# Delta-rule attention step: the result as two quarter-array products summed in PSUM, and every burst on two lanes of quarters

## The chip, the cores and the metric

The kernel runs on one core of a Trainium2 chip. The metric is device time in microseconds (us) of one execution, lower is better. TensorE (PE in the views) multiplies; VectorE (DVE), ScalarE (ACT) and GpSimd (POOL) do the elementwise work; SyncE (SP) starts most of the transfers. The 128x128 array of TensorE can be used as a whole or as four quarters of 64x64, each of which takes its own small product.

## The reference

Three stages in a row, all in fp32. Cut to what is computed:

```python
def _attn_ref(q, k, v, beta):            # (4 batches, 8 heads, 768 steps, 48)
    k_n = k / (norm(k) + 1e-06)
    state = zeros((B, H, D, D))
    for t in range(S):
        y[:, :, t] = einsum('bhd,bhde->bhe', q[:, :, t], state)
        v_old = einsum('bhde,bhd->bhe', state, kt)
        state = state + bt * einsum('bhd,bhe->bhde', kt, vt - v_old)

x = y.transpose(0, 2, 1, 3).reshape(3072, 384)

h = x @ w_in                              # MoE1: 384 -> 2048 -> 384
P = a[0] + a[1]*h + a[2]*h*h + a[3]*h*h*h
Q = 1.0 + abs(b[0])*abs(h) + abs(b[1])*h*h
x = (P / (Q + 1e-06)) @ w_out

h = x @ w_in                              # MoE2, own weights
r = maximum(h, 0.0)
return (r * r) @ w_out
```

## The kernel before, in words

**Attention.** The 768 steps of each batch are cut into 12 chunks of 64. A chunk of one batch is a "step" n = 4c + b (c the chunk, b the batch), 48 in all; eight steps form a group g = 0 to 5. The eight heads stand as four pairs p; the two heads j of a pair lie on rows 0 to 63 and 64 to 127 of a tile. Inside a chunk the recurrence is a triangular solve: a Gram matrix of the keys (`gram`), its inverse by 32x32 blocks (the loop of 31 steps, L497 and L501, on DVE for group 0 and on POOL for the others), and then for each step these products per pair and head:

- `kv`: keys times [queries | state], 64x112, into a PSUM tile H. Its left part is the scores, which are masked to a triangle; its right part is subtracted from the values (`cr`, L711).
- `tv`: inverse times the corrected values, 64x48, into U, which is copied out as the new values.
- the result Y: masked scores times new values, plus queries times state. Before, both lie below one another in a tile X, so that one product over 112 or 128 rows (`c3`, L727 for the one head, L728 for the other) forms the sum. X has two slots per batch, one per head, and zeros between the used rows.
- `ku`: keys times new values, 48x48, added to the state by DVE (`so`, L745).

`products` (L662) issues the quarter products of a burst two by two in turn from each kind. The scores are copied from PSUM head by head (`either`, which is ACT at L348 or DVE at L352, as the planner likes) and masked by POOL (L700); for chunk 1 alone DVE does copy and mask in one (L704).

**MoE1 and MoE2.** Six blocks i of 512 tokens by 16 tiles j of 128 hidden columns make 96 "units" in each. A unit of MoE1 is mm1 (L910, on split operands xh and xl), a rational function in 11 operations over ACT, DVE and POOL (L927 to L937, in this order of need: Abs, L928, L930 on POOL, L933, L934, L935, L936, L937; the cubic by `either` at L348 or L353, L931, L932, L935), and mm2 into three accumulators, either in fp32 (L958) or on split operands (L961, after L941 and L942). MoE2 has relu squared (L975 to L979) and L988 to L990.

**The order.** Nothing is scheduled by a compiler. A planner in the file (class `Plan`) takes every operation with an estimated duration, a due time (`tm(u)` = T0 + U1 u for unit u), reads, writes and a PSUM bank from a pool, runs a list schedule and issues every engine's instructions in the order found. Group 0 of the attention runs before MoE1; groups 1 to 5 run inside it, each as ten "bursts" t = 0 to 9, in which PE does `kv` of step t, `tv` of step t-1, the result and `ku` of step t-2 and, for the groups 1 to 3, one `gram` of a later group. Weights of MoE2 are prepared on DVE (L853, L861) and ACT in MoE1's last part. In idle stretches ahead of MoE1 the planner adds dummy products of `ones` (L303).

Of the kernel before, what the change touches and what calls it, by code (L numbers as in the profile page):

```python
# [19 lines left out]
C = 64  # L20
# [11 lines left out]
T0, U1, U2 = 88.0, 5.9, 4.15  # L32
# [213 lines left out]
def kernel(ctx, tc, kT, kS, qT, kn, vn, beta, par_in, w1, w2, outT):  # L246
# [13 lines left out]
    acc = banks[0:3]  # L260
    PL.pool("h", banks[3:6])
# [107 lines left out]
    for b in range(B):  # L369
        def xz(b=b):  # L370
            x = X[b]
            P_.memset(x[32:64, 1, :, 0:64], 0.0)
            P_.memset(x[64:128, 0, :, 64:112], 0.0)
            P_.memset(x[0:64, 1, :, 64:112], 0.0)
        add("POOL", 0.9, xz, w=[("q", b), ("q1", b), ("S", b)], due=10 + b, lock=1)

# [30 lines left out]
    for n in range(8):  # L407
# [42 lines left out]
    def attention(g):  # L450
# [36 lines left out]
        add("DVE", 2.2, r1, r=GB + ["nby", "be"], w=["nbr", "nrm"], due=d0, lock=1, after=turned if g == 1 else [])  # L487
        add("DVE", 0.2, lambda: V.transpose(nT[g % 2], nrm), r=["nrm"], w=[("nT", g % 2)], due=d0 + 2, lock=1)
        add("DVE", 1.3, lambda: V.tensor_tensor(Gb, Gb, _mid(nbr, [128, 32, 32]), op=ALU.mult), r=["nbr"], w=GB, due=d0, lock=1)
        add("DVE", 0.25, lambda: V.tensor_copy(Tt.rearrange("p a b -> p (a b)")[:, 0:1024:33], nbr), r=["nbr"], w=[tt], due=d0, lock=1)  # L490
        for s in range(31):
# [33 lines left out]
        if g < 2:  # L525
# [3 lines left out]
            add("POOL", 2.0, tz, w=[("TT", g)] + [("Dg", n) for n in range(8)] if g == 0 else [("kt0", q) for q in range(4)] + [("TT", 1)],  # L529
                due=d1 - 2, lock=1)  # L530
# [74 lines left out]
        def head(k):  # L605
# [20 lines left out]
        def kv(k):  # L626
# [17 lines left out]
        def ku(k):  # L644
# [480 lines left out]
```

## Time and profile before

| what | before |
|---|---|
| median of 3 runs | 1069.54 us (1068.82 to 1070.16) |
| profiled execution | 1065.81 us, its span 1064.1 us |
| mean granted clock of TensorE | 0.974 |
| PE busy | 1009.4 us of the span (95%) |
| DVE busy | 711.3 us (67%) |
| ACT busy | 625.6 us (59%) |
| POOL busy | 470.6 us (44%) |

The time of an execution is its span and what lies around it. Up to about 90 us PE does group 0 of the attention; MoE1 then runs to about 664 us and MoE2 to the end. Busy time of PE includes stretches at the lower of its two clocks: `PEclk` 1.00 is 2.4 GHz, 0.50 is 1.2 GHz, and a mean between them says which share of the stretch ran at either.

### The profile page before, as it was taken

Reading aid. Unit: us, or ns where it says so; the run is one execution under the profiler, and the core shown is the slowest. Engines: PE = TensorE matmul, PEld = TensorE weight load, DVE = VectorE, ACT = ScalarE, POOL = GpSimd, SP = SyncE. Lnnn points to the kernel's source line nnn. Section 1 sums busy time; section 2 is a strip of 40 time slices with the busy share of each in tenths; the row PEclk is TensorE's granted clock in tenths of the full one; section 3 lists DMA queues with packets and bytes.
Section 4 is the critical chain, followed back from the end, with each engine's and each line's share of the span. In section 5 each row is a group of like instructions: output and inputs, shape, how many; then the busy total and the mean of one; then the engine's idle time right before and its main releaser. Section 6 shows DMA issues by size and latency. Waiting matters only on the chain.

```text
span 1064.1 us, 22303 instructions
## 1 busy us (share of the span) xinstructions
PE 1009.4 (95%) x8932; PEld 755.7 (71%) x8932; DVE 711.3 (67%) x1154; ACT 625.6 (59%) x1126; POOL 470.6 (44%) x629
## 2 busy tenths in 40 slices
PE   5687998999999989999999898999999999999998
PEld 5575665567777766776766565888888888888886
DVE  4986888987898778778887998864343343433432
ACT  5364777777787877678776686753233242333322
POOL 3389999589868838873443453740000000000000
PEclk7978999999999999999999998999999999999999
DMA  7784367513731560251103113701010010000000
GB/s 245 185 214 104 86 185 228 88 36 104 169 72 38 148 104 34 67 127 37 28 9 123 59 60 127 259 1 59 1 30 30 1 60 1 1 30 1 30 0 30
DMA packets 126024, 85.44 MB, mean 80 GB/s; under 512 B 93344, under 2 KB 110880, under 8 KB 125920
## 3 DMA queue, kind: packets, MB, share of 16 engines
q1 hardware_dynamic: 125920, 84.02, 29.0%
q8 instruction: 70, 1.15, 0.4%
q14 instruction: 34, 0.28, 0.1%
HBM read 64.20 MB, written 18.61 MB: 78 GB/s over the span
## 4 chain that ended last, share of the span: by engine, by line
PE 72%; DVE 13%; POOL 7%; ACT 3%; issue 2%; DMA 2%; SPq 1%; POOLq 0%; DVEq 0%; ACTq 0%
PE bank L910 32%; PE bank L958 10%; PE bank L990 6%; PE bank L988 6%; PE bank L989 6%; PE bank L961 6%; PE bank L662 4%; POOL tmp L497 2%; POOL Tt L501 2%; PE bank L727 1%; DVE mem L937 1%; DVE mem L931 1%; DVE mem L932 1%; DVE mem L935 1%; DVE mem L353 1%
## 5 line engine op out<-in xcount | busy, mean ns | idle before, releaser
L910 PE MATMUL bank<-xh,A 128*128 128x512 f32 x1152 | 359.6, 393 | 1.0 <-POOL A L867 1.0
L910 PEld LDWEIGHTS bank<-xh,A 128*128 128x128 f32 x1152 | 218.2, 190 | 59.3 <-issue 11.3
L910 PE MATMUL bank<-xl,A 128*128 128x512 f32 x576 | 250.2, 434 | 6.6 <-DVE xl L894 3.4
L958 PE MATMUL bank<-mem,B 128*128 128x512 f32 x366 | 183.0, 621 | 17.4 <-DVE mem L937 17.4
L930 POOL TENSOR_TENSOR mem<-mem 128x512 f32<-128x512 f32 x96 | 125.4, 1306 | 110.9 <-ACT mem L928 108.9
L976 DVE SCALAR_TENSOR_TENSOR mem<-bank,mem 128x512 f32<-128x512 f32 x96 | 66.2, 690 | 147.4 <-ACT mem L975 147.3
L975 ACT ACTIVATE mem<-bank 128x512 f32<-128x512 f32 x96 | 57.4, 598 | 150.7 <-PE bank L910 150.7
L910 PEld LDWEIGHTS bank<-xl,A 128*128 128x128 f32 x576 | 109.3, 190 | 48.3 <-issue 10.4
L958 PEld LDWEIGHTS bank<-mem,B 128*128 128x128 f32 x366 | 68.2, 194 | 70.2 <-issue 41.8
L979 DVE TENSOR_TENSOR gl<-mem,gh 128x512 fp32r<-128x512 f32 x96 | 71.9, 749 | 65.4 <-ACT gh L978 65.3
L990 PE MATMUL bank<-gh,C 128*128 128x512 f32 x288 | 113.8, 395 | 0.0
L988 PE MATMUL bank<-gl,C 128*128 128x512 f32 x288 | 113.5, 394 | 0.0
L989 PE MATMUL bank<-gh,C 128*128 128x512 f32 x288 | 111.9, 389 | 0.0
L978 ACT CAST gh<-mem 128x512 fp32r<-128x512 f32 x96 | 59.6, 621 | 78.0 <-DVE mem L976 66.4
L501 POOL TENSOR_TENSOR Tt<-Tt,tmp 128x31 f32<-128x31 f32 (+15 forms) x155 | 88.0, 568 | 10.6
L497 POOL TENSOR_TENSOR tmp<-Gb,Tt 128x31 f32<-128x31 f32 (+15 forms) x155 | 84.6, 546 | 14.2 <-DVE Tt L490 4.6
L927 ACT ACTIVATE mem<-bank 128x512 f32<-128x512 f32 x96 | 57.1, 595 | 46.3 <-PE bank L910 24.2
L935 DVE SCALAR_TENSOR_TENSOR mem<-mem,par,bank 128x512 f32<-128x512 f32 x96 | 71.2, 742 | 17.5 <-ACT bank L934 16.5
L933 ACT ACTIVATE mem<-mem,par 128x512 f32<-128x512 f32 x96 | 69.2, 722 | 22.0 <-POOL mem L930 20.7
L928 ACT ACTIVATE mem<-mem,par 128x512 f32<-128x512 f32 x96 | 78.1, 814 | 2.7
L348 ACT COPY X<-bank 64x192 f32<-64x192 f32 (+1 forms) x176 | 59.3, 337 | 27.0 <-PE bank L662 12.4
L932 DVE SCALAR_TENSOR_TENSOR mem<-mem,par,bank 128x512 f32<-128x512 f32 x96 | 71.3, 744 | 4.3 <-ACT mem L927 1.9
(128 smaller groups left out, 1798.8 us busy)
## 6 DMA issues: line engine op xcount, KB each, us to landing
raw<-in_w_dram SPq DMA_DIRECT2D x18, 768.0 KB, 5.3
B<-in_w_dram SPq DMA_DIRECT2D x10, 768.0 KB, 5.7
kTg<-in_kS_dram SPq DMA_DIRECT2D x40, 128.0 KB, 2.6
gs<-Gs SPq DMA_DIRECT2D x40, 128.0 KB, 2.6
kTc<-in_kT_dram SPq DMA_DIRECT2D x40, 128.0 KB, 2.7
kn<-in_kn_dram SPq DMA_DIRECT2D x12, 384.0 KB, 3.9
X<-in_qT_dram SPq DMA_DIRECT2D x96, 48.0 KB, 2.8
vn<-in_vn_dram SPq DMA_DIRECT2D x12, 384.0 KB, 4.8
```

Source lines behind the costliest of these rows:

```text
L497: E_.tensor_tensor(tv, _mid(Gb[:, s, s + 1:32], [128, a, b]), Tt[:, 0:a, s:s + 1].to_broadcast([128, a, b]), op=ALU.mult)
L501: E_.tensor_tensor(Tt[:, 0:a, s + 1:32], Tt[:, 0:a, s + 1:32], tv, op=ALU.subtract)
L910: M.matmul(h, a, b, start=(k == 0 and m == 0), stop=(k == NK - 1 and m == 2))
L928: add("ACT", 0.83, lambda: A_.activation(b(), a(), AF.Identity, bias=s(4), scale=s(5)), r=[ak, "par"], w=[bk], due=due + 3.3, alloc=(("b", ...
L930: add("POOL", 1.32, lambda: P_.tensor_tensor(b(), b(), a(), op=ALU.mult), r=[ak], w=[bk], due=due + 4.2, lock=1)
L932: add("DVE", 0.75, lambda: V.scalar_tensor_tensor(c(), c(), s(1), h(), op0=ALU.add, op1=ALU.mult), r=[hk, "par"], w=[ck], due=due + 6.3)
L935: add("DVE", 0.75, lambda: V.scalar_tensor_tensor(c(), c(), s(0), h(), op0=ALU.add, op1=ALU.mult), r=[hk, "par"], w=[ck], due=due + 8)
L958: M.matmul(acc[d], Bw[j][:, e], slot[gk], start=(j == 0), stop=(j == NJ - 1))
L979: add("DVE", 0.72, lambda: V.tensor_tensor(gl(), b(), gh(), op=ALU.subtract), r=[bk, gk, "late"], w=[lk], due=due + 5, lock=1, alloc=(("gl ...
L988: M.matmul(acc[d], wh, gl, start=(j == 0), stop=False)
L989: M.matmul(acc[d], wl, gh, start=False, stop=False)
L990: M.matmul(acc[d], wh, gh, start=False, stop=(j == NJ - 1))
```

## The change

- **The result.** `c3` goes. In its place stand `mu` (new values times masked scores, 64 rows) and `qs` (state times queries, 48 rows), both quarter products, that add up in the same PSUM bank; only the first of a bank clears it.
- **X.** Slot 0 holds scores and new values of both heads, slot 1 queries and state. The zeros between go (12 memsets on POOL), the two query loads of a step become one of 112 KB, the two copies of U become one, the two additions to the state one.
- **The mask.** One DVE operation of 128x4x64 per step copies and masks the scores of both heads; the 88 maskings on POOL go.
- **The lanes.** `products` takes two lanes. `kv`, `tv` and `ku` use the quarters on the diagonal, `gram`, `mu` and `qs` the two others (the heads swap sides for that; the rows of w1 are permuted on the host). All products of a burst are issued in the order of their lane's columns so far. `gram` goes to the bank of Y, the state's product to that of U.
- **Planner.** U1 5.9 to 5.7, IV1 25 to 30, a factor SLOW 1.25 on the POOL inversion of group 1, SA 60 to 40 (the weights of MoE2 are prepared later), several durations; the last block's mm1 may also use the attention's banks, and its cubic always goes to ACT. The zeros of the second TT tile are copied by ACT from the first in place of two memsets.

```diff
-T0, U1, U2 = 88.0, 5.9, 4.15
+T0, U1, U2 = 88.0, 5.7, 4.15
+SLOW = 1.25
-IV1, WB, WS = 25, 44, 4.5
-SA, SB = 60, 4
+IV1, WB, WS = 30, 44, 4.5
+SA, SB = 40, 4
...
-                yield t[64:128, p, 0:w], kt[0:48, p], x[0:48, 1, p, 0:w]
-                yield t[0:64, p, 0:w], kt[64:112, p], x[64:112, 0, p, 0:w]
+                for o in (0, 64):
+                    yield t[o:o + 64, p, 0:w], kt[o:o + 48, p], x[o:o + 48, 1, p, 0:w]
...
-        def products(*gens):
-
-            gens = list(gens)
-            while gens:
-                for q in list(gens):
-                    for _ in range(2):
-                        y = next(q, None)
-                        if y is None:
-                            gens.remove(q)
-                            break
-                        M.matmul(*y, start=True, stop=True)
+        def products(*lanes):
+
+            seq = []
+            for q, lane in enumerate(lanes):
+                z = 0.0
+                for y in lane:
+                    z += y[0].free_size() if hasattr(y[0], "free_size") else y[0].shape[-1]
+                    seq.append((z, q, len(seq), y))
+            for *_, y in sorted(seq, key=lambda v: v[:3]):
+                a, z = y[3:] or (True, True)
+                M.matmul(*y[:3], start=a, stop=z)
...
-                add("POOL", 0.47, cm, r=["mark"] if c == 0 else [], w=[("M", b, j)], due=due + 0.5, lock=1)
+
+            def cp():
+                V.tensor_tensor(x[:, 0, :, 0:64], ps(hk, [128, NP, 112])[:, :, 0:64], _mid(tri, [128, NP, C]), op=ALU.mult)
+            add("DVE", 0.38, cp, r=[hk, "tri"], w=[("M", b)], due=due, free=[hk])
...
-        def c3(n):
+        def mu(k):
+            n = 8 * g + k
             t, x = yv(n), X[n % B]
             for p in range(NP):
-                M.matmul(t[0:48, p], x[0:112, 0, p, 64:112], x[0:112, 0, p, 0:64], start=True, stop=True)
-                M.matmul(t[64:112, p], x[:, 1, p, 64:112], x[:, 1, p, 0:64], start=True, stop=True)
+                for o in (0, 64):
+                    yield t[64 - o:112 - o, p], x[o:o + 64, 0, p, 64:112], x[o:o + 64, 0, p, 0:64], p == 0, n < B and p == NP - 1
+
+        def qs(k):
+            n = 8 * g + k
+            t, x = yv(n), X[n % B]
+            for p in range(NP if n >= B else 0):
+                for o in (0, 64):
+                    yield t[64 - o:112 - o, p], x[o:o + 48, 1, p, 64:112], x[o:o + 48, 1, p, 0:64], False, p == NP - 1
...
             def go():
-                if k2 is not None:
-                    c3(8 * g + k2)
-                products(*([kv(k0)] if k0 is not None else []), *([tv(k1)] if k1 is not None else []),
-                         *([ku(k2)] if k2 is not None else []), *([gram(m, slot["U", m - 16][:, NP * D:NP * (D + C)].rearrange("r (p c) -> r p c", p=NP))] if m else []))
+                products(chain(*([] if k0 is None else [kv(k0)]), *([] if k1 is None else [tv(k1)]), *([] if k2 is None else [ku(k2)])),
+                         chain(*([gram(m, slot["Y", g, t][:, NP * C:2 * NP * C].rearrange("r (p c) -> r p c", p=NP))] if m else []),
+                               *([] if k2 is None else [mu(k2), qs(k2)])))
...
-        either(0.78, 0.7, lambda: (c(), h()), s(2), s(3), r=[hk, "par"], w=[ck], due=due + 4.5, alloc=(("c",), ck))
+        if i == NT - 1:
+            add("ACT", 0.78, lambda: A_.activation(c(), h(), AF.Identity, bias=s(2), scale=s(3)), r=[hk, "par"], w=[ck], due=due + 4.5, alloc=(("c",), ck))
+        else:
+            either(0.78, 0.7, lambda: (c(), h()), s(2), s(3), r=[hk, "par"], w=[ck], due=due + 4.5, alloc=(("c",), ck))
```

What the new order looks like at three places (the names are those of the two programs; a tile's number only tells tiles apart).

POOL at the start of MoE1, before: the last steps of the inversion of group 1 (L497, L501), a weight (L867), the two memsets of TT (L528), and only then the first unit's product (L930).

```order
96 L497 TENSOR_TENSOR tmp_122<-Gb_118,Tt_120 128x60
97 L501 TENSOR_TENSOR Tt_120<-Tt_120,tmp_122 128x30x2
98 L497 TENSOR_TENSOR tmp_122<-Gb_118,Tt_120 128x31
99 L501 TENSOR_TENSOR Tt_120<-Tt_120,tmp_122 128x31
100 L867 TENSOR_TENSOR A_82<-mem,A_82 128x384
101 L528 MEMSET TT_115 32x32x32 x2
102 L930 TENSOR_TENSOR mem<-mem 128x512
```

POOL at the same place now (the inversion is L493 and L497, the unit's product L937):

```order
72 L493 TENSOR_TENSOR tmp_127<-Gb_123,Tt_125 128x156
73 L497 TENSOR_TENSOR Tt_125<-Tt_125,tmp_127 128x26x6
74 L937 TENSOR_TENSOR mem<-mem 128x512
75 L493 TENSOR_TENSOR tmp_127<-Gb_123,Tt_125 128x135
76 L497 TENSOR_TENSOR Tt_125<-Tt_125,tmp_127 128x27x5
77 L493 TENSOR_TENSOR tmp_127<-Gb_123,Tt_125 128x112
78 L937 TENSOR_TENSOR mem<-mem 128x512
```

The first two units' products have moved ahead of the last five steps of the inversion, and the memsets have left POOL there.

PE in a full burst of the groups 1 to 3, before: eight products of the result, then the quarters two by two.

```order
722 L727 MATMUL bank_73<-X_111 48x64
723 L728 MATMUL bank_73<-X_111 48x64
724 L727 MATMUL bank_73<-X_111 48x64
725 L728 MATMUL bank_73<-X_111 48x64
726 L662 MATMUL bank_76<-X_113,kTc_140 64x112 x2
727 L662 MATMUL bank_75<-vn_136,TT_115 64x48 x2
728 L662 MATMUL bank_73<-X_111,kn_134 48x48 x2
729 L662 MATMUL bank_75<-kTg_141 64x64 x2
```

PE in the same kind of burst now (all of it is L663):

```order
769 L663 MATMUL bank_74<-kTg_147 64x64 x2
770 L663 MATMUL bank_73<-X_115,kTc_142 64x112
771 L663 MATMUL bank_74<-kTg_147 64x64 x2
772 L663 MATMUL bank_73<-X_115,kTc_142 64x112
773 L663 MATMUL bank_74<-kTg_147 64x64
774 L663 MATMUL bank_73<-X_115,kTc_142 64x112
775 L663 MATMUL bank_74<-kTg_147 64x64 x2
776 L663 MATMUL bank_73<-X_115,kTc_142 64x112
777 L663 MATMUL bank_74<-X_117 48x64 x2
```

The products on whole rows are gone, and the two lanes alternate from the burst's first product on.

PE at the end of MoE1, before: the last units' mm2 (L961 on split operands, L958 in fp32), and behind all of them the first mm1 of MoE2 (L910 of A_79).

```order
2428 L961 MATMUL bank_71<-ph,F_2554 128x512
2429 L961 MATMUL bank_71<-ph,E_2547 128x512
2430 L958 MATMUL bank_69<-mem,B 128x512
2431 L958 MATMUL bank_70<-mem,B 128x512
2432 L958 MATMUL bank_71<-mem,B 128x512
2433 L910 MATMUL bank_76<-xl_99,A_79 128x512
2434 L910 MATMUL bank_76<-xh_96,A_79 128x512 x2
```

PE at the end of MoE1 now (mm1 is L914, mm2 L965 and L968):

```order
2854 L965 MATMUL bank_69<-mem,B 128x512
2855 L965 MATMUL bank_70<-mem,B 128x512
2856 L965 MATMUL bank_71<-mem,B 128x512
2857 L914 MATMUL bank_76<-xl_104,A_84 128x512
2858 L914 MATMUL bank_76<-xh_101,A_84 128x512 x2
2859 L914 MATMUL bank_76<-xl_105,A_84 128x512
2860 L914 MATMUL bank_76<-xh_102,A_84 128x512 x2
2861 L914 MATMUL bank_76<-xl_106,A_84 128x512
2862 L914 MATMUL bank_76<-xh_103,A_84 128x512 x2
2863 L968 MATMUL bank_69<-pl,E_2579 128x512
```

MoE2's first mm1 (A_84) now stands ahead of the last two units' mm2 of MoE1, and its second ahead of the last one's.

## Rows read from the trace of the kernel before

**Rows 1.** The page: span, and busy time of each engine.

```profile
span 1064.1 us, 22303 instructions
PE 1009.4 (95%) x8932; PEld 755.7 (71%) x8932; DVE 711.3 (67%) x1154; ACT 625.6 (59%) x1126; POOL 470.6 (44%) x629
```

**Rows 2.** Busy time of each engine by stretches; the first column is the stretch.

```profile
core 0: us, PE busy (x) PEld busy (x) DVE busy (x) ACT busy (x) POOL busy (x), PEclk, DMA share, GB/s
...
150.00:200.00 50.00, 45.42 (x585) 28.31 (x584) 45.17 (x73) 37.95 (x72) 38.86 (x53) 1.00 0.80 210
200.00:220.00 20.00, 17.96 (x179) 11.13 (x178) 19.03 (x32) 15.52 (x28) 15.19 (x22) 0.91 0.18 52
...
565.00:600.00 35.00, 31.01 (x106) 20.07 (x104) 26.53 (x40) 20.89 (x33) 10.29 (x8) 0.95 0.27 93
600.00:640.00 40.00, 38.88 (x143) 26.27 (x142) 39.17 (x56) 32.43 (x52) 21.77 (x18) 1.00 0.24 79
640.00:664.00 24.00, 19.79 (x59) 11.45 (x58) 21.06 (x30) 14.03 (x25) 8.72 (x8) 0.86 0.38 125
664.00:1064.00 400.00, 396.42 (x1728) 324.01 (x1726) 164.77 (x229) 151.49 (x255) 32.62 (x26) 1.00 0.11 36
```

**Rows 3.** Waits of PE from 88 to 660 us: total, times, longest.

```profile
PE bank L958 <- DVE mem L937: 17.4, 7, 4.6
```

**Rows 4.** Timeline of PE at MoE1's start: start, length, what, wait before.

```profile
90.00 0.79 PE L910 MATMUL bank<-xl,A 128*128 128x512 f32 x1 [3.43 <-DVE xl L894]
...
97.01 0.39 PE L910 MATMUL bank<-xl,A 128*128 128x512 f32 x1
...
99.07 3.12 PE L303 MATMUL bank<-ones 128*128 128x256 bf16 x27
106.77 3.39 PE L958 MATMUL bank<-mem,B 128*128 128x512 f32 x4 [4.58 <-DVE mem L937]
```

**Rows 5.** Timeline of POOL at the same place.

```profile
93.18 0.50 POOL L501 TENSOR_TENSOR Tt<-Tt,tmp 128x156 f32<-128x156 f32 x1
...
99.93 1.94 POOL L528 MEMSET TT<- 32x1024 f32 x2
101.95 1.27 POOL L930 TENSOR_TENSOR mem<-mem 128x512 f32<-128x512 f32 x1
```

**Rows 6.** Timeline of ACT at the same place: the first unit's L928.

```profile
94.98 0.81 ACT L928 ACTIVATE mem<-mem,par 128x512 f32<-128x512 f32 x1
```

**Rows 7.** Timeline of PE over a full burst with `gram`.

```profile
331.53 0.26 PE L727 MATMUL bank<-X 112*48 112x64 f32 x1
...
331.63 0.22 PE L728 MATMUL bank<-X 128*48 128x64 f32 x1
...
331.97 0.22 PE L728 MATMUL bank<-X 128*48 128x64 f32 x1
332.12 0.32 PE L662 MATMUL bank<-X,kTc 48*64 48x112 f32 x2
...
333.43 0.50 PE L961 MATMUL bank<-pl,E 128*128 128x512 f32 x1
```

**Rows 8.** Busy time of the quarter products (L662) in three bursts.

```profile
332.10:333.43 1.33, 1.31 (x64) 1.00 0.00 0
422.90:423.83 0.93, 0.92 (x32) 1.00 0.00 0
131.47:132.57 1.10, 1.09 (x48) 1.00 0.00 0
```

**Rows 9.** Groups of DVE instructions by shape: count, busy, mean ns.

```profile
L353 DVE TENSOR_SCALAR mem<-bank,par 128x512 f32<-128x512 f32 x56 | 45.2, 807 | 34.2 <-ACT mem L927 14.8 <-PE bank L910 14.5 <-POOL A L867 3.7
L745 DVE TENSOR_TENSOR X<-X,bank 48x192 f32<-48x192 f32 x96 | 33.7, 351 | 8.0 <-ACT xin L348 5.2 <-PE bank L662 0.7 <-ACT bank L934 0.4
...
L704 DVE TENSOR_TENSOR X<-bank,tri 64x256 f32<-64x256 f32 x8 | 3.4, 420 | 0.7 <-PE bank L662 0.6
```

**Rows 10.** Timeline of PE: the last wait of MoE1.

```profile
653.70 5.49 PE L958 MATMUL bank<-mem,B 128*128 128x512 f32 x6 [3.96 <-DVE mem L937]
```

More of the change, by code (lines that the diff above doesn't have):

```diff
@@ L1 @@
 import heapq
+from itertools import chain
 from contextlib import ExitStack
@@ L260 @@
     acc = banks[0:3]
+    for bank in banks[3:]:
+        nc.vector.memset(bank[32:64], 0.0)
     PL.pool("h", banks[3:6])
@@ L367 @@
     add("POOL", 0.6, corner, w=["tri"], due=14, lock=1)
[L369 to L375, printed above, removed]
     def step_due(n):
@@ L528, in tz, with tc_ @@
                     P_.memset(t[64 * j + 32:64 * j + 64, :, :, 0:32], 0.0)
-            add("POOL", 2.0, tz, w=[("TT", g)] + [("Dg", n) for n in range(8)] if g == 0 else [("kt0", q) for q in range(4)] + [("TT", 1)],
-                due=d1 - 2, lock=1)
+            add("POOL", 2.0, tz, w=[("TT", 0), "zero"] + [("Dg", n) for n in range(8)], due=d1 - 2, lock=1)
+        if g == 1:
+            def tc_(j, t=TTg):
+                o = 64 * j + 32
+                return t[o:o + 32, :, :, 0:32].rearrange("r s p c -> r (s p) c"), TT[0][o:o + 32, :, :, 0:32].rearrange("r s p c -> r (s p) c")
+            for j in range(2):
+                either(1.1, 0.75, lambda j=j: tc_(j), r=["zero"], w=[("kt0", q) for q in range(4)] + [("TT", 1)], due=d1 - 2)
         TTv = TTg.rearrange("r s p c -> r (s p) c")
@@ L682, in first @@
                 r += [("TTx", g % 2, i, j) for i in range(2) for j in range(2)] + ([("TT", g % 2)] if g < 2 else [])
-                w, al = w + [("U", n2)], al + [(pl, ("U", n2))]
+                w, al = w + [("U", n2)], al + [(pl, ub(k2, 1))]
             def go():
-                products(*([kv(k)] if k is not None else []), *([tv(k2)] if k2 is not None else []))
+                products(chain([] if k2 is None else tv(k2)), chain([] if k is None else kv(k)))
             add("PE", 1.05 if k is None else 0.95 if 8 * g + k >= B else 1.05, go, r=r, w=w, due=due, alloc=al, free=fr)
@@ L760, in rest, with go @@
             ucopy(k, due)
-            add("PE", 0.62, lambda: c3(n), r=cin(b), w=[yk], due=due + 2, alloc=(pl, yk))
-            add("PE", 0.55, lambda: products(ku(k)), r=[("Us", b, 0), ("Us", b, 1), ("kn", c % 2), yk], w=[dk], due=due + 3)
+            def go():
+                products(ku(k), chain(mu(k), qs(k)))
+            add("PE", 0.95, go, r=cin(b) + [("kn", c % 2)], w=[yk, dk], due=due + 2, alloc=(pl, yb(k)))
             result(k, due)
         def burst(t, due):
-            r, w, al, fr, dur = [], [], [], [], 0.0
+            r, w, al, fr = [], [], [], []
             k0, k1, k2 = (x if 0 <= x < 8 else None for x in (t, t - 1, t - 2))
@@ L781, in burst @@
                 r += [("TTx", g % 2, i, j) for i in range(2) for j in range(2)] + ([("TT", g % 2)] if g < 2 else [])
-                w, al = w + [("U", n)], al + [(("att", "h"), ("U", n))]
+                w = w + [("U", n)]
+            if t:
+                al = al + [(("att", "h"), ("U", g, t))]
+            if m or k2 is not None:
+                al = al + [(("att", "h"), ("Y", g, t))]
             if m:
@@ L978, in relu2 @@
         add("ACT", 0.62, lambda: A_.copy(gh(), b()), r=[bk, "late"], w=[gk], due=due + 4.2, alloc=(("gh",), gk))
-        add("DVE", 0.72, lambda: V.tensor_tensor(gl(), b(), gh(), op=ALU.subtract), r=[bk, gk, "late"], w=[lk], due=due + 5, lock=1,
+        add("DVE", 0.76, lambda: V.tensor_tensor(gl(), b(), gh(), op=ALU.subtract), r=[bk, gk, "late"], w=[lk], due=due + 5, lock=1,
             alloc=(("gl",), lk), free=[bk])
@@ L1065, in prep_attn @@
     kT = np.zeros((NSS, 128, NP, C), np.float32)
-    kT[:, 64:112] = kt[:, 0]
-    kT[:, 0:48] = kt[:, 1]
+    kT[:, 0:48] = kt[:, 0]
+    kT[:, 64:112] = kt[:, 1]
     kS = np.zeros_like(kT)
-    kS[:, 0:48] = kt[:, 0]
-    kS[:, 64:112] = kt[:, 1]
+    kS[:, 64:112] = kt[:, 0]
+    kS[:, 0:48] = kt[:, 1]
+    qt = tr(q)
+    qT = np.zeros((NSS, 112, NP, C), np.float32)
+    qT[:, 0:48] = qt[:, 0]
+    qT[:, 64:112] = qt[:, 1]
     def nat(x):
@@ L1092, in prep_inputs @@
     for k in range(NK):
-        for j in range(2):
+        for j in (1, 0):
             rows += range(D * (2 * k + j), D * (2 * k + j + 1))
```

96 lines of the change are left out of this document (41 added, 55 removed).

## The prediction

> **What bounds the kernel now.** I read the page first: PE is busy 1009.4 us of a span of 1064.1 [rows 1], so what the change can bring lies in the other 55 us, in stretches at the lower clock, and in PE's own work. Next the busy time by stretches. From 664 us on PE works 396.42 of 400 us at full clock while DVE has 164.77 [rows 2]: MoE2 is PE's alone, the change leaves its products as they are, and I count it as unchanged. Inside MoE1 PE is full too, but for a few places: it idles 4.6 us in 150 to 200, 2.0 in 200 to 220, and 4.0, 1.1 and 4.2 in the three stretches from 565 to 664; and where PEclk is below 1.00 part of the stretch ran at 1.2 GHz in place of 2.4, of which a stretch of length W loses W(1 - PEclk): 20 x 0.09 = 1.8 us, 35 x 0.05 = 1.75 and 24 x 0.14 = 3.4 [rows 2]. Where PE waited, the waits tell for whom: seven times, 17.4 us together, an mm2 in fp32 waited for L937, the end of a unit's rational function [rows 3]. So three things can move the time: PE's work in the bursts, how early that chain ends at MoE1's start, and how much DVE, ACT and POOL have beside the chain where PE is close to starving. At 150 to 220 DVE is busy 64.2 of 70 us and at 600 to 640 39.17 of 40 [rows 2]; there it, not PE, is the limit.
>
> **The change part by part.**
>
> *MoE1's start.* PE's first mm1 begins at 90.00; two mm1 are through at 97.01, the third at 99.07, then come 27 dummies of 3.12/27 = 0.116 us and a wait of 4.58 until the first mm2 at 106.77 [rows 4]. The first unit's L928 ended at 94.98 + 0.81 = 95.8 [rows 6], but its L930 stood in POOL's order behind the whole inversion of group 1 and two memsets (1.94 us) and began at 101.95 [rows 5]. From that start to mm2 it took 106.77 - 101.95 = 4.82 us. In the new order L930 (now L937) stands behind the inversion step whose last part ended at 93.18 + 0.50 [rows 5], so it can start with its operands at 95.8, and mm2 at 95.8 + 4.82 = 100.6. PE's order may be later: two mm1, 39 dummies (4.5 us) and the third mm1 (99.07 - 97.01 = 2.06) stand before the mm2, which gives 97.01 + 4.5 + 2.06 = 103.6 if the first mm1 runs as slowly as before. (That slowness is the lower clock, behind the wait of 3.43 us for xl, and 9 more dummies now stand ahead of it.) The gain is between 3.2 and 6.2 us; if xl comes up to 1.3 us earlier too, since one query load in place of two stands in SP's queue, up to 7.5. I take **-5.3**, near the middle. What is pushed back, the last five inversion steps and the TT zeros, is wanted only by `tv` in the bursts, which first ran at 131.47 [rows 8]; the zeros now cost ACT two copies of a kind that POOL did in 0.97 each.
>
> *The bursts.* In the full burst the result's records follow one another in pairs: from the second L728 at 331.63 to the eighth at 331.97 are six slots, 57 ns each for 64 columns, 0.89 ns a column; the whole burst took 333.43 - 331.53 = 1.90 us, 0.59 of it the result [rows 7]. Every product is two records. If a quarter costs the larger of its columns and its weights' columns at that price, `kv` costs 2 x 112 x 0.89 = 0.20 us per pair of heads, `tv`, `gram`, `mu` and `qs` 0.114 each, `ku` 0.085. That reproduces the rows: 4 x 0.20 and a drain of 0.13 give 0.93 for `kv` beside `tv`, measured 0.92; 4 x (0.20 + 0.085) + 0.13 = 1.27 for all four kinds, measured 1.31 [rows 8]. The new lanes are 4 x (0.20 + 0.114 + 0.085) = 1.60 and 4 x 3 x 0.114 = 1.37, side by side, so a full burst takes 1.60 + 0.13 = 1.73 to 1.75: -0.15 for each of 30. Burst t = 1 gets slower, since `kv` and `tv` now share a lane: 4 x 0.314 + 0.13 = 1.39 in place of 0.92 (twice) and 1.09 (three times) [rows 8], +1.8 together. t = 8 and 9 lose the result's own time and gain a lane of 1.37 or 0.91, some -0.9 in all. Sum -4.5 + 1.8 - 0.9 = -3.6. Bounds: if records can't be issued faster than the 1.31/64 = 20.5 ns of now [rows 8], a full burst of 96 records takes 1.97 + 0.13 = 2.10 in the 18 with `gram` and 1.77 in the 12 without, in all +0.2 x 18 - 0.13 x 12 + 1.8 - 0.9 = +2.9; below, 0.05 us better each, -5. I take **-3.0**, near the column price, which two rows bear out.
>
> Against this stands a rule of the Trainium skill: by "TensorE: Matmul & The Clock Gate", Part 1, section "Wait — 56ns, not 53.3ns?", starts of matmuls never come closer than about 25 ns, however small they are. By it 96 records would need 2.4 us, an estimate from that page, and the bursts would cost some +14 us in place of -3.0. The trace disagrees, 20.5 ns a record over 64 of them [rows 8], so I give it little.
>
> *The load beside PE.* DVE gets the mask: 48 operations of L704's length along the rows, but on 128 rows, where it did 8 of 64 rows. That the rows cost nothing I read from L353, 128 rows at 807/512 = 1.6 ns an element of a row, beside L704's 420/256 = 1.6 [rows 9]. So 40 x 0.42 = +16.8 (3 less if the plain copies of scores that DVE did are counted). It loses 96 - 44 = 52 additions to the state at 0.351, -18.3, and 24 of 56 cubics at 0.807, -19.4 [rows 9]. Together -21 us of the 711.3 - 164.8 = 546 it has before 664 [rows 1, 2]. At 150 to 220, where PE loses 6.6 us idle and 1.8 to the clock [rows 2], that share of 64.2 is 2.5 us, and the chain from scores to result loses a hop over POOL: I take **-3.0**, bounds 0 and -8.4 (all of it).
>
> *MoE1's last block.* Here PE loses 4.0 + 1.1 + 4.2 = 9.3 us idle and 1.75 + 3.4 = 5.1 to the clock that fell behind the waits, 14.4 together [rows 2]. All 16 cubics go to ACT; if DVE did its average share of 56 in 96, nine of them, it loses 7.5 us there [rows 9], out of 86.8 in 99 [rows 2]. Part of MoE2's weights moves behind the end of MoE1 too. ACT takes on what DVE loses, and with 32.43 of 40 [rows 2] it has room. The six records of mm2 that waited 3.96 [rows 10] now have an mm1 of MoE2 ahead of the ones behind them, so PE's gap there is filled with work that is due anyway. I leave a start-up dip of 2 us and an end of 3, 5 of 14.4: **-9.4**, bounds 0 and -14.4.
>
> *At nothing:* the memsets that leave POOL (44% busy [rows 1]) and the five new ones on DVE stand at the kernel's start beside loads; if that cover fails, they are a us or two. The 88 maskings off POOL and 124 copies off ACT lay beside PE's own work.
>
> *Sum:* -5.3 - 3.0 - 3.0 - 9.4 = -20.7. The profiled execution (span 1064.1 and 1.7 around it) would take 1045.1; the median of the runs stands 3.7 above it, and the same difference gives **1049 us**.
>
> **The rivals.**
>
> *A, the last block stays as it is.* For it: DVE is full at 600 to 640 [rows 2], and ACT's added 0.8 us a unit lengthens the chain that ends in L937. Against: DVE's share falls by more. The first three terms stand: 1069.5 - 11.3 = 1058.
>
> *B, all of PE's holes close.* The 15.9 us idle and 6.9 at the lower clock of the five stretches [rows 2] go, beside MoE1's start and the bursts. For it speaks that PE has an mm1 to fill with nearly everywhere; against, that each block's first units must pass the whole chain. 1069.5 - 5.3 - 5 - 22.8 = 1036.
>
> *C, slower: the quarters of a lane take turns.* Now two heads' products of one kind write the same PSUM bank from two halves of the rows in both lanes, all burst long. If they, or the two lanes, can't run side by side, the full burst takes 1.60 + 1.37 + 0.13 = 3.1 us, 1.2 more for each of 30, +36; less the other 17.7 that is +18: 1088. It decides from a burst of 1.90 + 17.7/30 = 2.5 us on. Against: `kv` of two heads does the same already, and 32 records of `kv` and `tv` took 0.92 us where one after another 16 x 0.10 + 16 x 0.057 = 2.5 would be needed [rows 8]. The Trainium skill's "TensorEngine Tiling (Array Packing)", Gotcha 1, says that row tiles cannot access the same PSUM bank at the same time, which would make this the forecast; by that row the trace disagrees.
>
> *D, MoE2's weights come too late.* They are prepared 20 us later; if DVE is behind by that, the first block of MoE2 waits: up to 1049 + 20 = 1069. The order puts six of eight ahead of MoE2's first relu.
>
> *E, the issue bound* of the 20.5 ns: +2.9 in place of -3.0, 1055.
>
> **How the numbers follow.** Forecast 0.55 (own range 1043 to 1054), A 0.18, B 0.09, C 0.05, D 0.05, E 0.08. Leaving out C, half of D and half of B, the range is 1038 to 1062. A measurement of this kernel tells about 0.2% (2 us) from no change. Slower is C and a part of D: 0.07; the same, a part of D: 0.03; faster the rest: 0.90.
>
> **What would show it.** Right: the first mm2 between 100 and 104 us; a full burst of 1.7 to 1.8 us with both lanes starting together; PE's waits for the last product of a unit below 10 us in all; MoE2 some 396 us of work in 400. Wrong: a full burst above 2.1 us (the lanes), PE idle over 10 us from the last block's start to MoE2, or MoE2's PE waiting for B or C weights.

## The result and the profile after

The changed kernel takes 1050.63 us (median of 4 runs, 1049.59 to 1050.7), the kernel before 1069.53 (4 runs): a ratio of 0.982, 95% interval 0.980 to 0.984, or 18.9 us less. The forecast was 1049, and the time lies inside its range. The sum held better than its terms did, though, and that is luck in part, as the section on the prediction shows.

The page of the changed kernel, against [rows 1]:

```profile
span 1049.0 us, 23443 instructions
PE 1005.8 (96%) x9684; PEld 760.8 (73%) x9684; DVE 674.8 (64%) x1100; ACT 601.6 (57%) x1043; POOL 427.2 (41%) x527
```

PE's busy time fell by 3.6 us only, the span by 15.1: what went is mostly time in which PE stood still. (The other 3.8 of the 18.9 are no gain of the trace: the first profile of the kernel before was a quick execution. A second one had a span of 1067.8, 18.8 above.) DVE lost 36.5 us, POOL 43.4.

Busy time by the same stretches as in [rows 2], as far as MoE1 goes, and two more (107 to 150 and 220 to 330), columns as there. First these two in the kernel before:

```profile
107.00:150.00 43.00, 43.00 (x644) 27.48 (x645) 35.02 (x55) 31.86 (x58) 39.75 (x55) 0.97 0.42 104
220.00:330.00 110.00, 110.00 (x1271) 78.36 (x1270) 92.94 (x158) 88.52 (x160) 90.81 (x128) 1.00 0.36 87
```

and all of them now:

```profile
107.00:150.00 43.00, 41.10 (x690) 26.51 (x689) 33.98 (x56) 31.22 (x54) 40.14 (x52) 1.00 0.59 146
150.00:200.00 50.00, 46.63 (x797) 30.72 (x797) 42.00 (x76) 37.67 (x69) 36.91 (x44) 1.00 0.85 207
200.00:220.00 20.00, 18.59 (x62) 11.06 (x61) 15.98 (x25) 16.51 (x28) 14.97 (x26) 1.00 0.11 41
220.00:330.00 110.00, 108.10 (x1352) 76.87 (x1354) 84.59 (x144) 78.88 (x135) 81.09 (x108) 0.98 0.34 85
...
565.00:600.00 35.00, 34.99 (x133) 24.60 (x132) 24.54 (x36) 26.03 (x42) 13.66 (x10) 1.00 0.33 113
600.00:640.00 40.00, 39.13 (x138) 25.36 (x136) 38.88 (x54) 36.27 (x57) 19.54 (x15) 1.00 0.12 40
640.00:650.00 10.00, 9.34 (x34) 6.07 (x34) 9.93 (x13) 8.09 (x16) 8.05 (x7) 1.00 0.75 230
```

From 565 to MoE1's end at 650 PE idles 1.5 us at full clock, where it lost 14.4 before. DVE is as full there as it was (38.88 of 40); ACT took the cubics (36.27, before 32.43). But two stretches in which the kernel before had no idle PE now have some: 1.9 us at 107 to 150 (where it lost 0.03 x 43 = 1.3 to the clock before) and 1.9 at 220 to 330, the second with the lower clock for part of it.

PE's waits of the changed kernel from 80 to 660 us, against [rows 3] (columns as there):

```profile
PE bank L914 <- DVE xl L898: 5.0, 2, 4.3
PE bank L968 <- POOL pl L949: 3.4, 4, 1.9
PE bank L914 <- DVE mem L944: 3.1, 3, 1.6
...
PE bank L965 <- DVE mem L944: 0.8, 3, 0.3
```

The wait that led the list, an fp32 mm2 for the end of a unit's rational function (now L944), fell from 17.4 us to 0.8; what leads now is the first mm1's wait for xl, and smaller waits for the same chain.

PE at MoE1's start, against [rows 4]:

```profile
91.92 0.79 PE L914 MATMUL bank<-xl,A 128*128 128x512 f32 x1 [4.31 <-DVE xl L898]
...
98.69 4.43 PE L307 MATMUL bank<-ones 128*128 128x256 bf16 x39
104.29 0.50 PE L914 MATMUL bank<-xl,A 128*128 128x512 f32 x1 [1.17 <-DVE mem L944]
...
106.47 1.88 PE L965 MATMUL bank<-mem,B 128*128 128x512 f32 x4
```

The first mm1 came 1.9 us later than before, not earlier, and the first mm2 only 0.3 us earlier. What stands right ahead of that mm2 is the third mm1, which now stands behind the dummies and waited 1.17 us for L944, the end of the first unit; before, it ran ahead of the dummies at once [rows 4].

Busy time of the burst's products (L663) in four bursts, against [rows 7, 8]: a full one with `gram`, one without, and t = 1 without and with it.

```profile
338.30:340.09 1.79, 1.79 (x96) 1.00 0.07 18
425.04:426.79 1.75, 1.75 (x80) 1.00 0.03 9
421.93:423.30 1.37, 1.37 (x32) 1.00 0.00 0
329.75:331.14 1.39, 1.39 (x48) 1.00 0.00 0
```

Since mm1 always has nine records a unit, the start of every unit can be found in PE's timeline. Stretches in us, from the two profiles of each kernel (the second ones are runs e8 and e5 below); the last row ends where PE's last product starts:

| stretch | before | again | after | again |
|---|---|---|---|---|
| start to first mm2 | 106.8 | 109.3 | 106.5 | 104.8 |
| first mm2 to unit 16 | 92.4 | 92.6 | 92.0 | 91.1 |
| units 16 to 48 | 188.8 | 187.8 | 188.7 | 187.8 |
| units 48 to 80 | 189.4 | 191.1 | 185.2 | 185.3 |
| unit 80 to PE's last product | 482.7 | 482.9 | 472.5 | 473.9 |

Taken as means, that is -2.4, -1.0, -0.1, -5.0 and -9.6: half of the gain lies behind unit 80, where MoE1's last block is, and most of the rest in the third of MoE1 before it. The five add up to -18.1, beside 18.9 for the medians.

### The profile page after: what moved, and what is told of

It is laid out like the page before. It is cut to its first block, busy times and chain, and to the rows that moved or that the text cites. A ratio compares the mean times of both kernels' runs of the same rounds, so it can differ in the third digit from the quotient of the medians.

```text
span 1049.0 us, 23443 instructions
## 1 busy us (share of the span) xinstructions
PE 1005.8 (96%) x9684; PEld 760.8 (73%) x9684; DVE 674.8 (64%) x1100; ACT 601.6 (57%) x1043; POOL 427.2 (41%) x527
## 3 DMA queue, kind: packets, MB, share of 16 engines
q8 instruction: 76, 1.25, 0.5%
## 4 chain that ended last, share of the span: by engine, by line
PE 77%; DVE 11%; POOL 3%; DMA 3%; issue 2%; ACT 2%; SPq 1%; DVEq 0%; POOLq 0%; ACTq 0%
PE bank L914 33%; PE bank L965 11%; PE bank L663 7%; PE bank L997 6%; PE bank L995 6%; PE bank L996 6%; PE bank L968 5%; SPq L337 1%; DVE mem L939 1%; DVE mem L938 1%; DVE mem L944 1%; DVE mem L942 1%; DVE tmp L493 1%; DVE Tt L497 1%; DVE bank L943 1%
## 5 line engine op out<-in xcount | busy, mean ns | idle before, releaser
L914 PE MATMUL bank<-xh,A 128*128 128x512 f32 x1152 | 359.5, 393 | 1.5 <-POOL A L871 1.5
L914 PEld LDWEIGHTS bank<-xh,A 128*128 128x128 f32 x1152 | 217.8, 189 | 61.4 <-issue 13.1
L914 PE MATMUL bank<-xl,A 128*128 128x512 f32 x576 | 251.3, 436 | 9.4 <-DVE xl L898 5.0
L937 POOL TENSOR_TENSOR mem<-mem 128x512 f32<-128x512 f32 x96 | 124.9, 1301 | 153.7 <-ACT mem L932 152.5
L965 PE MATMUL bank<-mem,B 128*128 128x512 f32 x366 | 176.9, 601 | 0.8 <-DVE mem L944 0.8
L914 PEld LDWEIGHTS bank<-xl,A 128*128 128x128 f32 x576 | 109.2, 190 | 48.4 <-issue 9.6
L965 PEld LDWEIGHTS bank<-mem,B 128*128 128x128 f32 x366 | 66.4, 189 | 49.1 <-issue 39.1
L497 POOL TENSOR_TENSOR Tt<-Tt,tmp 128x31 f32<-128x31 f32 (+15 forms) x155 | 88.8, 573 | 10.4
L493 POOL TENSOR_TENSOR tmp<-Gb,Tt 128x31 f32<-128x31 f32 (+15 forms) x155 | 82.0, 529 | 11.6 <-DVE Tt L486 2.3
L938 DVE TENSOR_TENSOR mem<-bank,mem 128x512 f32<-128x512 f32 x96 | 65.9, 686 | 27.0 <-ACT mem L352 16.7
L939 DVE SCALAR_TENSOR_TENSOR mem<-mem,par,bank 128x512 f32<-128x512 f32 x96 | 71.6, 746 | 3.4 <-ACT mem L931 0.7
```

The source lines that it names most:

```text
L493: E_.tensor_tensor(tv, _mid(Gb[:, s, s + 1:32], [128, a, b]), Tt[:, 0:a, s:s + 1].to_broadcast([128, a, b]), op=ALU.mult)
L497: E_.tensor_tensor(Tt[:, 0:a, s + 1:32], Tt[:, 0:a, s + 1:32], tv, op=ALU.subtract)
L914: M.matmul(h, a, b, start=(k == 0 and m == 0), stop=(k == NK - 1 and m == 2))
L937: add("POOL", 1.32, lambda: P_.tensor_tensor(b(), b(), a(), op=ALU.mult), r=[ak], w=[bk], due=due + 4.2, lock=1)
L938: add("DVE", 0.69, lambda: V.tensor_tensor(c(), h(), c(), op=ALU.mult), r=[hk], w=[ck], due=due + 5.5)
L939: add("DVE", 0.75, lambda: V.scalar_tensor_tensor(c(), c(), s(1), h(), op0=ALU.add, op1=ALU.mult), r=[hk, "par"], w=[ck], due=due + 6.3)
```

## The experiments

Ten more kernels ran, and both kernels a second time, each against runs of the kernel before on the same chip (1069.9 to 1071.3 in the medians).

**e1, the lanes in turn.** All products of a burst's first lane, then all of the second; outside the bursts the order is the changed kernel's.

```diff
-            for *_, y in sorted(seq, key=lambda v: v[:3]):
+            for *_, y in seq:
```

> The changed kernel with one line undone: inside a burst all products of the first lane are issued, then all of the second, not sorted by columns; everything outside the bursts stands in the same order. Theory (two lanes run side by side on different quarters, priced by columns): a full burst takes 1.60 + 1.37 + 0.13 = 3.1 us in place of 1.79, +1.3 for 30 bursts and about +0.8 for each of the 13 smaller two-lane ones that overlap, in all some +40 to +50 us if PE's time is the kernel's time there, about 1093. Rival (a burst is bound by the issue of its 96 records, 1.79/96 = 18.6 ns each, so the order inside is of no account): burst 1.8, time 1050 to 1052.

1077.95 us (ratio 1.007, 1.006 to 1.009), 27 above the changed kernel. Its bursts, with `gram` and without (busy time of the products):

```profile
352.60:355.57 2.97, 2.97 (x96) 1.00 0.43 106
441.09:443.58 2.49, 2.49 (x80) 1.00 0.02 7
```

The same 96 records take 1.79 us side by side and 2.97 one lane after the other, which is 1.60 + 1.37 by the column price. So the lanes do run side by side, and the number of records is not what bounds a burst. The 27 are less than the expected 40: the full bursts cost 18 x (2.97 - 1.79) + 12 x (2.49 - 1.75) = 30 more, since without `gram` the second lane is short, and the first mm2 happened to begin 3.3 us earlier in this execution (103.16).

**e2, the last block's two edits undone.**

```diff
-            alloc=(("h",) if l == 1 and i < NT - 1 else ("h", "att"), hk))
+            alloc=(("h",) if l == 1 else ("h", "att"), hk))
...
-        if i == NT - 1:
-            add("ACT", 0.78, ...)
-        else:
-            either(0.78, 0.7, ...)
+        either(0.78, 0.7, ...)
```

> The changed kernel with only the two edits to MoE1's last block undone (the cubic goes to ACT or DVE as the planner likes, mm1 of the last block has three banks, not five). Theory (MoE1's last block gave the larger half of the gain: PE lost 13.5 us there before and 1.5 after): PE idles and runs at 1.2 GHz again between 550 and 660 us, 8 to 13 us lost, time 1058 to 1063. Rival (DVE's lighter load in the whole of MoE1 cleared the last block): PE still loses under 4 us there, time 1050 to 1053.

1054.38 us (0.985, 0.983 to 0.988), between the two ranges. From unit 80 to the end 477.7 us, halfway from 472.5 to 482.7. PE's waits in the last block, in the kernel before:

```profile
PE bank L958 <- DVE mem L937: 8.0, 2, 4.0
```

and in e2, where L962 is the mm2 and L941 the unit's end:

```profile
PE bank L962 <- DVE mem L941: 4.0, 1, 4.0
PE bank L965 <- POOL pl L946: 1.6, 2, 1.0
PE bank L914 <- DVE xl L898: 1.5, 1, 1.5
```

One of the two long waits is back, not both: the cubic and the banks together give half of the block's gain. No run parts these two.

**e7, MoE2's weights as early as before**, up to unit 80 in the changed kernel's order.

```diff
-SA, SB = 40, 4
+SA, SB = 60, 4
```

> The changed kernel with SA 60 in place of 40: MoE2's weights are prepared 20 us earlier, inside MoE1's last block; everything up to there stands in the same order. Theory (the later weights free DVE where it was full, and are worth half of what the last block gained): the stretch from unit 80 to the end takes 476 to 479 us in place of 472.5, time 1054 to 1057. Rival (the cubic on ACT and the banks alone do it): 472 to 474, time 1050 to 1052.

1053.24 us (0.984, 0.982 to 0.986), just under the expected range and 4.2 above the unaltered kernel of the same chip (e5). From unit 80 to the end 476.1. In its last block PE waits 3.3 us for another thing than before, MoE2's own first gl, and 2.3 for pl:

```profile
PE bank L995 <- DVE gl L986: 3.3, 1, 3.3
PE bank L968 <- POOL pl L949: 2.3, 1, 2.3
```

So the later weights are worth 2 to 4 us. **e12** went on in that direction:

```diff
-SA, SB = 40, 4
+SA, SB = 25, 4
```

> The changed kernel with SA 25 in place of 40: MoE2's weights are prepared another 15 us later. Theory (the later weights free DVE in MoE1's last block, of which 1.5 us idle and MoE2's 1.6 are left): at most 1 to 3 us less, 1047 to 1050. Rival (they then come too late): PE waits in MoE2 for weights, the stretch from unit 80 to the end over 475 us, 1052 to 1060.

1048.9 us (0.981, 0.979 to 0.984), beside 1049.03 for the unaltered kernel in e5; 474.0 from unit 80 on. No gain, no loss: the time that PE still idles in the block (1.5 us in the changed kernel) is not DVE's load of weights.

**e3 and e4, the change in two halves.** e3 is the kernel before with everything that the change does to the planner and to the last block; e4 the new attention with the planner and the last block as before. The planner's numbers, besides the durations and the last block's edits:

```diff
-T0, U1, U2 = 88.0, 5.9, 4.15
+T0, U1, U2 = 88.0, 5.7, 4.15
...
+SLOW = 1.25
...
-IV1, WB, WS = 25, 44, 4.5
-SA, SB = 60, 4
+IV1, WB, WS = 30, 44, 4.5
+SA, SB = 40, 4
...
```

> The kernel before with all that the change does to the planner's numbers and to MoE1's last block (U1 5.7, IV1 30, SA 40, SLOW 1.25, durations, cubic on ACT, banks), and the old attention. Theory (the last block is worth 12 us, the bursts 2, less load on DVE and POOL 3 to 5): 1053 to 1057. Rival (the attention's rewrite is what carries the gain): 1062 to 1068.

> The changed kernel with the planner's numbers and MoE1's last block as before, and the new attention. Theory: bursts as in the changed kernel (1.79 us), the last block's waits back, time 1060 to 1066. Rival (the attention's rewrite carries the gain): 1051 to 1055.

e3: 1060.42 (0.991, 0.990 to 0.993). e4: 1068.65 (0.998, 0.997 to 0.999). Alone the plan gives some 10 us and the attention under 2, together 19 (22 in e5). Neither expectation held in full. What did hold is the last block. PE's windows from unit 80 to MoE2's first mm2 (columns as in [rows 2]): the kernel before,

```profile
577.38:671.89 94.51, 85.18 (x300) 56.92 (x298) 83.45 (x115) 68.63 (x111) 44.02 (x36) 0.95 0.34 114
```

e4,

```profile
576.90:672.28 95.38, 84.62 (x300) 56.33 (x298) 84.10 (x112) 71.39 (x116) 47.64 (x38) 0.96 0.36 121
```

e3,

```profile
582.00:659.61 77.61, 76.11 (x282) 52.10 (x280) 69.81 (x96) 68.70 (x111) 39.44 (x31) 1.00 0.28 95
```

and the changed kernel.

```profile
572.40:650.01 77.61, 76.09 (x281) 52.09 (x280) 69.81 (x96) 68.70 (x111) 39.47 (x31) 1.00 0.27 91
```

(With the new plan fewer mm1 of MoE2 stand ahead of its first mm2, so the lengths themselves don't compare; PE's idle time does, 9.3 and 10.8 against 1.5 and 1.5, and so does the time from unit 80 to the end, 482.7 and 483.5 against 472.5 and 472.5.) The last block belongs to the plan alone, to the tenth. The extra 8 us of the two together lie ahead of unit 16. It begins at 199.2 us (202.0 in e8) with the old attention and plan, at 206.1 with the new plan alone, at 200.2 with the new attention alone, and at 198.5 (195.9 in e5) with both. Behind unit 16 the sums agree, but not stretch by stretch: units 48 to 80 took 190.4 us in e3 and 188.0 in e4, beside 185.2 with both.

**e11** asked whether the new numbers on group 1's inversion are what the old attention can't bear: e3 with SLOW and IV1 as before.

```diff
-SLOW = 1.25
-IV1, WB, WS = 30, 44, 4.5
+SLOW = 1.0
+IV1, WB, WS = 25, 44, 4.5
```

> The old attention with the new plan, but the two numbers on group 1's inversion (SLOW, IV1) as before. Theory (the old attention with the new plan lost 8 us up to unit 16, because its inversion and its maskings on POOL compete there, and POOL was busy 19 of 20 us from 130 to 190): with the inversion first, unit 16 begins at 198 to 202 us, not at 206.1, and the time is 1053 to 1057. Rival (the attention's old form itself holds the first block back): unit 16 at 205 or later, 1059 to 1062.

1062.27 us (0.993, 0.991 to 0.994), unit 16 at 204.5 us: by these two numbers the rival holds. But the stretches tell otherwise. From the first mm2 to unit 16, e3 and then e11:

```profile
108.13:206.13 98.00, 90.36 (x1352) 57.11 (x1350) 79.89 (x131) 71.93 (x132) 82.41 (x109) 0.97 0.67 164
```
```profile
113.18:204.50 91.32, 88.64 (x1354) 56.32 (x1353) 79.34 (x131) 70.46 (x131) 79.04 (x102) 1.00 0.58 155
```

With the inversion first, the block takes 91.3 us in place of 98.0, no longer than in the kernel before (92.4) or the changed one (92.0). So the old attention's form by itself does not hold the block back, and the theory's reason fits the block. What e11 loses it loses ahead of the block: its first unit's product on POOL (L934) came behind the inversion and the memsets, PE waited 9.2 us for that unit's end (L941), and its first mm2 began 5 us later than in e3:

```profile
104.35 2.59 POOL L934 TENSOR_TENSOR mem<-mem 128x512 f32<-128x512 f32 x2
109.17 0.79 PE L911 MATMUL bank<-xl,A 128*128 128x512 f32 x1 [9.22 <-DVE mem L941]
```

So with the old attention the two numbers move a loss of 5 to 7 us from the start to the block or back. Why the old attention with the new plan reaches unit 16 6 to 10 us behind the changed kernel either way is not shown: no run put the mask, the memsets or the lanes alone on top of e3.

**e9, L937's place on POOL.** The same two numbers in the changed kernel, by which the first unit's product goes back behind the inversion.

> The changed kernel with the planner's two numbers on group 1's inversion undone (SLOW 1.0, IV1 25). The order then puts the first unit's product (L937) behind the whole inversion and four weights on POOL, as in the kernel before; from 220 us on it is nearly the changed kernel's order. Theory (at MoE1's start the gain comes from L937's place on POOL alone, and it is 3 to 5 us): first mm2 at 107.5 to 110.5 us, in place of 103.2 to 106.5 in the four profiles of the changed order, time 1052 to 1055. Rival (the start is held by xin's transfer, L937's place is of no account): first mm2 at 104 to 106.5, time 1049 to 1051.

The first mm2 began at 109.74, as the theory had it; the time was 1049.99 (0.981, 0.978 to 0.984), as the rival had it. Its two stretches of MoE1's start:

```profile
91.66:109.74 18.08, 14.71 (x59) 11.54 (x60) 13.01 (x25) 9.60 (x12) 16.43 (x30) 0.69 0.59 161
109.74:197.93 88.19, 85.96 (x1464) 55.69 (x1463) 71.75 (x120) 67.24 (x120) 68.03 (x80) 0.99 0.61 157
```

The mm2 came 3 us later than in the changed kernel and unit 16 no later (197.93; 198.50; 195.89 in e5): what the start gains, the block behind it largely gives back, as between e11 and e3.

**e5, e8: both kernels a second time.**

> The changed kernel unaltered, profiled a second time beside the ones below on the same chip. Theory (MoE1's first mm1 hangs on the transfers ahead of xin in SP's queue, which take differently long from run to run): the start of the first mm1 differs from 91.92 us by 1 to 3 us, as in the two experiments with the same order up to there (89.57 and 90.37), while the stretch from unit 80 to the end stays within 1.5 us of 472.5. Rival: the start is fixed by the order, 91.9 within 0.3.

> The kernel before unaltered, profiled a second time. Theory (the first profile, 1065.8 us, was 3.7 below the median because MoE1 began early in it): the first mm1 begins at 91 to 95 us, not 90.0, and the stretch from the first mm2 on is as long as before within 1.5 us. Rival: the difference lies spread over MoE1 and MoE2.

e5: 1049.03 us (1047.58 to 1053.49), its first mm1 at 90.06, not 91.92, and 473.9 from unit 80 on. e8: 1069.51 in its one run, its first mm1 at 88.58, but the first mm2 at 109.33. So the head differs by 1.4 to 2.6 us between executions of one kernel, in both. The part of e8's expectation on the first mm1 was wrong; of the 3.7 us to the first profile 2.6 lie ahead of the first mm2, and from there on the two differ by 1.1, as expected.

**e6, xin ahead of Gb in SP's queue.** In the changed kernel SP's transfers at that place are (start, time in issue):

```profile
82.99 3.77 SPq L337 DMA_DIRECT2D Gb<-gs  x4
86.81 1.33 SPq L337 DMA_DIRECT2D xin<-xin  x2
```

The last copy into xin had ended at 82.94, so xin's transfer waited for four others that were waiting themselves, until 82.9, for the last store of gs to land.

```diff
-                        r=[("gs", 8 * g + ss) for ss in range(8)], w=[("Gb", q, o)], due=d0 - 3)
+                        r=[("gs", 8 * g + ss) for ss in range(8)], w=[("Gb", q, o)], due=d0 - 3, after=turn3 if g == 2 else [])
...
+                    if n == 7:
+                        turn3.append(i3)
```

> The changed kernel with one more dependence in the plan: group 2's four Gb<-gs loads stand behind the two xin transfers in SP's queue, not ahead. Theory (xin waits in SP's queue behind Gb<-gs, which itself waits for the last gs store to land): the xin transfer is issued right after the last copy into xin ends, 3 to 4 us earlier, the first mm1 begins 2.5 to 3.5 us earlier and the time falls by 1.5 to 3.5 us, 1047 to 1049. Rival (the start is held by something else, POOL's inversion or the lower clock): first mm1 earlier, but the first mm2 not, time within 1 us of the changed kernel.

1050.32 us (0.981, 0.979 to 0.983), no gain. The plan put four query loads in the place of Gb's:

```profile
80.27 4.33 SPq L337 DMA_DIRECT2D X<-in_qT_dram  x4
84.69 1.22 SPq L337 DMA_DIRECT2D xin<-xin  x2
```

The transfer was issued at 84.69, beside 84.33 in e5, and the first mm1 began at 91.14. The run moved the queue but not the transfer, so it says nothing on what an earlier xin would give; by e9 one would expect little.

**e10, the due times as far apart as before.**

```diff
-T0, U1, U2 = 88.0, 5.7, 4.15
+T0, U1, U2 = 88.0, 5.9, 4.15
```

> The changed kernel with U1 5.9 in place of 5.7, the planner's due times 0.2 us a unit later. Theory (PE's own work sets the pace between MoE1's blocks, a due time only picks among what is ready): units 16 to 80 take 373 to 376 us as in the changed kernel (373.0 to 373.9), time 1049 to 1052. Rival (the due times pace the bursts, a slower plan leaves PE idle): 64 units lose up to 0.2 us each, 377 or more, time 1054 to 1062.

1052.95 us (0.983, 0.982 to 0.985); units 16 to 80 in 375.8 us, from unit 80 on 474.1. By the stretch the theory holds, by the time neither does: a slower plan costs some 2 us in these units, and a loss in the time (1.3 to 2.7 us by the ratios) is not clear of what the runs differ by. Units 48 to 80 took 186.8.

No run beat the changed kernel by more than its runs differ.

## Why the prediction was right, point by point

*What bounds the kernel.* Right: MoE2 stayed full but for 1.6 us of waits for its A weights, and the gain came out of PE's idle time in MoE1.

*MoE1's start, -5.3: the step that failed.* The first mm2 was to begin between 100 and 104 us; it began at 106.47, and at 104.81 in e5. L937 did move ahead of the inversion's last five steps (the second unit's ahead of three and a half of them), but it then waited for its operands until 97.79, since the first mm1 came at 91.92 and not at 90.0 or earlier. From there the first unit's chain did not take the 4.82 us of before: L944 ended at 104.24, 6.45 us after L937's start, with an operation of the second unit (L939) right ahead of it on DVE.

```profile
97.79 1.29 POOL L937 TENSOR_TENSOR mem<-mem 128x512 f32<-128x512 f32 x1 [8.15 <-ACT mem L932]
102.71 0.74 DVE L939 SCALAR_TENSOR_TENSOR mem<-mem,par,bank 128x512 f32<-128x512 f32 x1
103.55 0.69 DVE L944 SCALAR_TENSOR_TENSOR mem<-bank,mem 128x512 f32<-128x512 f32 x1
```

The bound worked from PE's order (103.6) was the one that mattered, and it lacked a wait. Two mm1 were through at 98.69, not 97.01, which is 1.7 us, and the third mm1, which stands ahead of the mm2, waited 1.17 for that L944. In e5, whose first mm1 began at 90.06 as forecast, the wait is there too:

```profile
102.64 0.50 PE L914 MATMUL bank<-xl,A 128*128 128x512 f32 x1 [1.16 <-DVE mem L944]
```

Why xl was later, not earlier, in the first profile is not shown. In the new order Gb's four transfers stand right ahead of xin's on SP (e6), which the forecast had left out, but e6 did not move xin's transfer. Measured over two profiles each, -2.4 to the first mm2. And e9 shows that the term should not have been carried to the sum at all: with L937 back in its old place the kernel is as fast.

*The bursts, -3.0.* The mechanism was right, the size nearly: 1.79 and 1.75 us for 1.73 to 1.75; t = 1 took 1.37 and 1.39 for 1.39. Eighteen times -0.11, twelve times -0.15, three times +0.30 and twice +0.45 make -2.0. The bursts t = 8 and 9, for which the forecast had -0.9, gave 0.01 to 0.04 each, -0.3 in all; t = 8 with `gram`, before and now:

```profile
274.04:275.70 1.66, 1.66 (x66) 1.00 0.61 183
267.30:268.92 1.62, 1.62 (x82) 1.00 1.03 170
```

That is -2.3 together, where the terms had made -3.6 and -3.0 was taken. The rivals that bound a burst by its issue are out: 96 records in 1.79 us are 18.6 ns each, less than the 20.5 that I held against the Trainium skill's 25 ns ("TensorE: Matmul & The Clock Gate", Part 1, "Wait — 56ns, not 53.3ns?"). So products on different quarters start closer than that floor, on average over the burst. The other rule of the Trainium skill, that row tiles can't use one PSUM bank at the same time ("TensorEngine Tiling (Array Packing)", Gotcha 1), would have made the changed kernel as slow as e1 or slower; here two heads' products from two halves of the rows add up in one bank, all burst long, at the column price.

*The load beside PE, -3.0.* The three counts on DVE came out: 48 masks at 418 ns on 128 rows, 44 additions, 32 cubics. Its total fell by more, 36.5 us and not 21, since other work left it too (15 copies of Gs, 6.2 us, among it).

```profile
L357 DVE TENSOR_SCALAR mem<-bank,par 128x512 f32<-128x512 f32 x32 | 25.9, 808 | 21.1 <-ACT mem L931 17.7 <-PE bank L914 3.5
L702 DVE TENSOR_TENSOR X<-bank,tri 128x256 f32<-128x256 f32 x48 | 19.9, 418 | 7.1 <-PE bank L663 6.9
L743 DVE TENSOR_TENSOR X<-X,bank 112x192 f32<-112x192 f32 x44 | 15.4, 349 | 14.9 <-PE bank L663 10.5 <-ACT X L352 3.4 <-ACT Gs L352 0.9
```

The place did not. At 150 to 220 PE's loss fell from 8.4 to 4.8 us as forecast, but the waits came back ahead of it and behind it, and up to unit 48 nothing is left of it (the table above). A gain shows at units 48 to 80, -5.0, of which I had counted only the bursts' part, about 1. Neither half of the change gives it alone (190.4 in e3, 188.0 in e4), and some 1.6 of it hangs on U1 (186.8 in e10); that the rest is DVE's lighter load is not shown.

*The last block, -9.4.* Right in size, -9.6 to -10.2, and right in kind: e2 and e7 split it into two parts, the cubic on ACT with the two banks (5 us) and the later weights (2 to 4), and e3 shows that it needs nothing of the attention.

So -20.7 forecast and -18.9 found agree because the start's 3 us and the middle's 3 that did not come were in large part made up by 4 at units 48 to 80 that I had not counted: the mechanism is right for the last block and the bursts, and the closeness of the sum is luck. Rival A is refuted by the last block; B went too far, PE still idles 10 to 11 us from the first mm2 to MoE1's end; C by e1 and the bursts; D by e12; E by the bursts.

## What to carry to other kernels

Don't carry a gain at the start of a long pipeline to its end before looking at the next meeting point (here unit 16, which needs the attention of group 1); a gain in the last block can be carried, since little behind it can give it back. The small products on quarters cost here what their columns cost on their lane, so balance the lanes, not the number of products. And where a planner writes the order, test its numbers and the rewrite apart: here they gave 10 and 2 us alone and 19 together.

## What the runs showed of the hardware that was not expected

The lower clock doesn't follow every pause of the same size. In one execution of the kernel before, PE waited 2.04 us ahead of an mm2 at 214.62 and 2.06 us ahead of one at 398.25:

```profile
214.62 2.92 PE L958 MATMUL bank<-mem,B 128*128 128x512 f32 x4 [2.04 <-DVE mem L937]
398.25 2.84 PE L958 MATMUL bank<-mem,B 128*128 128x512 f32 x6 [2.06 <-DVE mem L937]
```

The ten us around the first have PEclk 0.83, so part of them ran at 1.2 GHz; those around the second have 1.00:

```profile
213.00:223.00 10.00, 8.38 (x67) 5.33 (x68) 8.04 (x14) 7.38 (x14) 7.07 (x13) 0.83 0.15 54
396.00:406.00 10.00, 7.94 (x29) 4.76 (x26) 8.90 (x15) 6.37 (x12) 6.36 (x15) 1.00 0.27 92
```

One such stretch costs 10 x 0.17 = 1.7 us, a good part of what runs of one kernel differ by (1.1 us among the changed kernel's four, 5.9 among e5's).
